# VectorE's share of the softmax exponentials: due passes ahead of the pass that waits for scores, and a higher threshold for taking score banks in the last layer

## The chip, the core and the metric

One core of a Trainium2 chip. The metric is the device time of one execution in microseconds; the kernel before takes 2177.55 us, the median of three runs (2173.53 to 2179.21).

## The reference

Four attention layers in a row on a tensor x of 2048 rows and 640 columns, 32 heads of 20 columns. Layers 0 and 2 look at a window of 256 keys (A), layers 1 and 3 at all 2048 keys (B).

```python
def _B_ref(x, wqkv, wo):
    qkv = (x @ wqkv).reshape(B, S, 3, H, Dh).transpose(2, 0, 3, 1, 4)
    q, k, v = qkv[0], qkv[1], qkv[2]
    scores = jnp.einsum("bhqd,bhkd->bhqk", q, k) * (Dh ** -0.5)
    p = _softmax(scores, axis=-1)
    o = jnp.einsum("bhqk,bhkd->bhqd", p, v)
    return o.transpose(0, 2, 1, 3).reshape(B, S, D) @ wo
# _A_ref: the same with scores masked to 0 <= q - k < 256
x = x + _A_ref(_layernorm(x), A_wqkv, A_wo)
x = x + _B_ref(_layernorm(x), B_wqkv, B_wo)
x = x + _A_ref(_layernorm(x), A_wqkv, A_wo)
x = x + _B_ref(_layernorm(x), B_wqkv, B_wo)
```

## The kernel before

The Python program writes every engine's instruction list out by hand. Queries come in 4 chunks of 512 rows (c), heads in 8 groups of 4 (g). A unit is one layer, chunk and group; a unit of a full layer has 64 score banks (16 blocks of 128 keys by 4 heads), and a bank is 128 keys by 512 queries, one of the eight PSUM banks. The main loop goes in steps (`tick`). Each step takes two to four banks from the current unit, issues their score matmuls (L1405), one ScalarE exponential over all of them (L1429), then the value matmuls of an earlier step (L1462) and a share of background work. Even steps use banks 0 to 2, odd ones 3 to 5 (and 6, where a step is four banks wide), bank 7 collects the output. Bank 6 is otherwise the one bank that the background shares (`take_m`, `drop_m`): layer norms, projections, the softmax denominators (`t_tail`: L1134, L1154, L1175) and output projections (`t_out`: L583). Each of these fills the bank with TensorE and has VectorE read it out. Idle places of TensorE are filled with matmuls that nobody reads (`unread`, in the profile as `ps<-masks,ident`).

ScalarE does most of the exponentials, and VectorE does a few in arithmetic of its own, two banks at a time: two fixed-point passes that read the scores from PSUM (`side_fixed`, L981, one for each bank), and then a chain on both banks: fraction (L997), square (L1005), cubic (L1009) and whole (L1015). In layer 1 the last two are cut in halves of 512 columns. Up to the first part of layer 3 (before `final`, the first unit of layer 3 with c = 1) the side bank is the third bank of a step's tile, whose exponential then covers two banks. From `final` on, `side_scores` computes it in bank 6 (L964), and the step keeps its three banks. `side["late"]` is set late in layer 3's first chunk.

Whether a step takes a side bank is decided by `state["lag"]`, the program's own account of how far VectorE is behind: each issued pass adds its length, each step takes off its ScalarE time. The account must be under `LAG` (late) or `LAG_1` (before). Chain passes are issued at the end of each step by `side_work(False)`, as long as the account stays within `WORK` or `WORK_1`. So in VectorE's order a fixed-point pass stands ahead of the chain passes of its own step.

Of the kernel before, what the change touches and what calls it, by code (L numbers as in the profile page):

```python
# [26 lines left out]
C = 512  # L27
# [9 lines left out]
LOG2E = 1.4426950408889634  # L37
T1, T0, TB = 3.219389291006841e-05, 3.290376630637895, -33.6189874849745
KA = 18
LAG = 0.5  # L40
LAG_1 = 0.5
WORK = 2.2
WORK_1 = 1.4
KEEP = 30
HALF = True
MOST_1 = 64
GAP_1 = 5
QA = 4
# [8 lines left out]
def kernel(  # L57
# [79 lines left out]
    def packed(l, c):  # L137

        return l == 3 and c > 0
# [55 lines left out]
    ready = set()  # L195
    todo = []
    tails = []
    state = {"tick": 0, "held": None, "credit": 0.0, "early": True, "act": True, "unit": 0, "heat": 0.0, "carry": 0.0, "least": 0.0, "floor": 0.0, "owed": 0, "lag": 0.0}

    class Task:  # L200

# [48 lines left out]
    def choose(blocked, limit=1 << 30):  # L250
        if state["held"] is not None:
            return state["held"]
        for t in tails:
            if t.wake <= state["tick"]:
                return t
        if not blocked:
            for t in todo:
                if t.wake <= state["tick"] and (t.need <= limit or t.holds):
                    return t
        return None  # L260
# [13 lines left out]
    mfree = {5: (0, 0), 6: (0, 1)}  # L274
    mseq = [1]

    def take_m():
        while True:
            b = min(mfree, key=mfree.get)
            if mfree[b][0] <= state["tick"]:  # L280
                mfree[b] = (1 << 30, 0)
                return b
            yield ("wait", 1)

    def drop_m(b):
# [9 lines left out]
    def require(what):  # L295
        n = 0
        while what not in ready:
            n += 1
            assert n < 100000, what
            t = choose(False, state["unit"] if n < 400 else 1 << 30)  # L300
            if t is None:
                state["tick"] += 1
                continue
            state["credit"] = max(state["credit"] - advance(t), -1.0)
# [444 lines left out]
    early = deque(Unit(1, 0, g, p) for p in PARTS[1][:3] for g in range(G))  # L749
# [109 lines left out]
    def finish_unit(u):  # L859
        l, c, g = u.l, u.c, u.g  # L860
        state["lag"] += 0.7
        if u.part and u.part[1] < NT:
            if not part_o:
                part_o["t"] = big.tile([P, G, C], F32, name="raw_o", tag="early_late")
            raw_o = part_o["t"][:, g, :]
            if u.part[0] == 0:
                nc.vector.tensor_copy(out=raw_o, in_=op)
            else:
                nc.vector.tensor_tensor(out=raw_o, in0=raw_o, in1=op, op=ALU.add)
            return  # L870
        if (l, c) not in ons:
            for ll, cc in list(ons):
                if len(ons) >= 2:
                    require(("out", ll, cc))
            ons[l, c] = onp.tile([P, G, C], BF16, name="on", tag="on")
        while len(tails) >= 3:
            require(tails[0].name)
        end = (l, c) == (3, NC - 1) and g >= G - 2
        oT = ons[l, c][:, 5 + g % 3 if packed(l, c) and not end else g, :]
        if u.part:  # L880
            nc.vector.tensor_tensor(out=oT, in0=part_o["t"][:, g, :], in1=op, op=ALU.add)
        else:
            nc.vector.tensor_copy(out=oT, in_=op)  # L883
        ended_units.append((l, c, g, oT))
        if len(ended_units) == 2 or g == G - 1 or end :
            push_tail(("tail", l, c, g), t_tail(list(ended_units)))
            ended_units.clear()
# [4 lines left out]
    side = {  # L892
        "xi": deque(), "chain": deque(), "out": deque(), "late": False, "early": False,
        "half": None, "at": 0, "last": 0,
    }
# [29 lines left out]
    def side_giver():  # L925
# [9 lines left out]
        for n in range(side["at"], min(side["at"] + 3, len(givers))):  # L935
# [3 lines left out]
            if not side["late" if u.l == 3 else "early"]:  # L939
                return None  # L940
            if u.l == 1 and len(u.aside) >= MOST_1:
                continue
            if len(u.rest) >= (KEEP if len(u.rest) + len(u.aside) < u.size else 12):
                side["at"] = n
# [13 lines left out]
    def side_scores(u):  # L958

        mseq[0] += 1  # L960
        mfree[6] = (state["tick"] + 2, mseq[0])
        kc, j = side_take(u)
        z = ps[:, 6, :]
        nc.tensor.matmul(z, lhsT=u.k(kc, j), rhs=u.q(j, 0, 4), start=True, stop=True)  # L964
        side_fixed(z)

    def side_fixed(z):

        u, a, b = side["half"]
        i = 0 if b is not None else 1  # L970
        if i == 0:
            side["now"] = side["xi"].popleft()
            side["half"] = (u, b, None)
        else:
            side["half"] = None
            if id(u) in deferred:
                live["kt"] -= 1
                live["qt"] -= 1
        xi = side["now"]
        side["last"] = state["tick"]  # L980
        nc.vector.tensor_scalar(  # L981
            out=xi.bitcast(I32)[:, i * C : (i + 1) * C], in0=z,
            scalar1=SCALE * LOG2E * FIX, scalar2=127.5 * FIX, op0=ALU.mult, op1=ALU.add,
        )
        state["lag"] += 0.7
        if i == 1:
            side["chain"].append(chain(u, xi))

    def chain(u, xi):

        V = nc.vector
        t = side["t"]
        low = xi.bitcast(I16)[:, 0::2]
        box = {}

        def fraction(h):
            V.tensor_scalar(  # L997
                out=t[:, h], in0=low[:, h], scalar1=T1, scalar2=T0, op0=ALU.mult, op1=ALU.add
            )

        def square(h):
            if "out" not in box:
                box["out"] = side["out"].popleft()
            q = box["q"] = box["out"].rearrange("p a b -> p (a b)").bitcast(F16)
            V.tensor_tensor(out=q[:, h], in0=t[:, h], in1=t[:, h], op=ALU.mult)  # L1005

        def cubic(h):
            q = box["q"]
            V.scalar_tensor_tensor(  # L1009
                out=q[:, h], in0=q[:, h], scalar=TB, in1=t[:, h], op0=ALU.add, op1=ALU.mult  # L1010
            )

        def whole(h):
            q = box["q"]
            V.scalar_tensor_tensor(  # L1015
                out=q.bitcast(U16)[:, h], in0=xi.bitcast(I32)[:, h], scalar=1.0 / C,
                in1=q[:, h], op0=ALU.mult, op1=ALU.add,
            )
            if h.stop == 2 * C:
                side["xi"].append(xi)  # L1020
                side_out.setdefault(id(u), []).append((box["out"], state["tick"]))

        every = (slice(0, 2 * C),)
        halves = (slice(0, C), slice(C, 2 * C)) if HALF and u.l == 1 else every
        cost = 0.7 if len(halves) == 2 else 1.25
        steps = [(fraction, h, 0.7) for h in every] + [(square, h, 0.7) for h in every]
        steps += [(cubic, h, cost) for h in halves] + [(whole, h, cost) for h in halves]
        return deque(steps)

    def side_work(force):  # L1030

        while side["chain"]:
            step, h, cost = side["chain"][0][0]
            if step.__name__ == "square" and not side["out"]:
                return False
            if not force and state["lag"] + cost > (WORK if side["late"] else WORK_1):
                return False
            side["chain"][0].popleft()
            if not side["chain"][0]:
                side["chain"].popleft()  # L1040
            step(h)
            state["lag"] += cost
            if force:
                return True
        return False
# [240 lines left out]
    with tc.manual_schedule():  # L1286
# [74 lines left out]
        while ended is None or t < ended + 8:  # L1361
            t += 1
            state["tick"] += 1
            n_b = 0
            if flow:
# [7 lines left out]
                if state["unit"] >= final:  # L1373
                    last_tick[0] = 0
                giver = side_giver() if state["lag"] < (LAG if side["late"] else LAG_1) else None
                if giver is not None and state["unit"] >= final and (
                    state["held"] is not None or mfree[6][0] > state["tick"]
                ):
                    giver = None
                cur = next_tile(t, giver)  # L1380
                n_b = len(cur)
                for b in cur:
                    u = b[0]
# [25 lines left out]
                if cur[-1][2] == "side":  # L1409
                    cur = cur[:-1]  # L1410
                    n_b -= 1
                    side_fixed(sp[:, n_b, :])
                elif giver is not None and state["unit"] >= final:
                    side_scores(giver)
                for b in cur:
                    if b[-1]:
                        s_emitted(b[0])
# [25 lines left out]
            for n in range(2 if n_b == 0 or t > closed + 1 else 0):  # L1443
                u = pts[0][3][0] if pts else None
# [6 lines left out]
                subs, end = group[0][3][4], group[-1][3][7]  # L1451
# [21 lines left out]
                if end:  # L1473
# [2 lines left out]
                    closed = t  # L1476
                    break

            if n_b and not state["early"]:
                background(t, n_b)  # L1480
            if n_b:
# [78 lines left out]
```

## Time and profile before

| what | value |
|---|---|
| median of three runs | 2177.55 us |
| the profiled execution | 2173.51 us |
| its span, first to last instruction | 2171.8 us |
| mean granted TensorE clock | 0.997 |
| side banks: layer 1, layer 3 (passes of L981 into raw_o, into xnT) | 112, 190 |

The span is the time from the first to the last instruction; about 1.7 us of the execution lie around it. Busy time is the union of an engine's spans, and a row's mean is that of single spans, which overlap: two exponentials that follow each other without a pause start 1.33 us apart, though each is recorded as some 1.5 us long. Layer 1 with layer 2 woven in takes about 450 to 1400 us of the span, layer 3's first chunk up to about 1540 us, and its other three chunks the rest.

### The profile page before, as it was taken

What the parts mean: (1) busy time and instruction counts of PE and PEld (TensorE: products, weight loads), DVE (VectorE), ACT (ScalarE), POOL (GpSimd) and SP (SyncE); (2) the same over time, 40 slices, a digit from 0 to 9 for tenths busy, and PEclk for the clock granted to TensorE, in tenths of its full rate; (3) what the DMA queues carried; (4) which work ended last, traced back from release to release, by engine and by line L of the source; (5) the groups of instructions that cost most, each with busy time, mean ns of one, the idle gap of its engine ahead of it and who ended that gap; (6) DMA issues with size and microseconds to landing.
All of it is one profiled execution on the core that took longest, in us unless ns stands there. A gap on an engine that the chain in (4) does not pass through costs nothing. (4 is left out here: it accounts for less than half of the span.)

```text
span 2171.8 us, 73321 instructions
## 1 busy us (share of the span) xinstructions
PE 1927.8 (89%) x31803; PEld 753.7 (35%) x31803; DVE 1443.6 (66%) x2564; ACT 2095.1 (96%) x1721; POOL 490.6 (23%) x952
## 2 busy tenths in 40 slices
PE   8899999988899888888988989888888888888888
PEld 4444443433333333333333433332222222222222
DVE  6656565426666676776777743676688778767876
ACT  7899899999999999999999999999999999999998
POOL 6665546110131213411053112511000000000000
PEclk9999999999999999999999999999999999999999
DMA  6233233332210323112241123122211111111100
GB/s 203 76 85 107 74 91 101 84 83 58 77 49 22 84 61 89 41 37 65 56 114 31 44 78 99 39 55 68 59 41 54 32 32 42 35 33 36 47 27 17
DMA packets 88418, 137.29 MB, mean 63 GB/s; under 512 B 20766, under 2 KB 63486, under 8 KB 88094
## 3 DMA queue, kind: packets, MB, share of 16 engines
q1 hardware_dynamic: 68878, 79.43, 13.8%
q0 software_dynamic: 19216, 53.17, 8.3%
q8 instruction: 249, 4.08, 0.8%
q14 instruction: 75, 0.61, 0.1%
HBM read 99.52 MB, written 27.79 MB: 59 GB/s over the span
## 5 line engine op out<-in xcount | busy, mean ns | idle before, releaser
L1429 ACT ACTIVATE pt<-ps 128x1536 bf16<-128x1536 f32 (+2 forms) x1641 | 2054.7, 1412 | 44.4 <-PE ps L1405 30.0
L1405 PE MATMUL ps<-qt,kt 32*128 32x512 bf16 x3930 | 546.1, 384 | 64.4 <-ACT pt L1429 57.0
L311 PE MATMUL ps<-masks,ident 128*32 128x512 bf16 x5696 | 503.4, 384 | 95.0 <-ACT pt L1429 50.4
L1462 PE MATMUL ps<-pt,vt 128*21 128x512 bf16 x3778 | 377.2, 386 | 0.5 <-ACT pt L1429 0.5
L1405 PEld LDWEIGHTS <-kt 32*128 32x128 bf16 x3930 | 156.2, 91 | 470.6 <-issue 452.1
L311 PEld LDWEIGHTS <-ident 128*32 128x32 bf16 x5696 | 178.4, 94 | 285.8 <-issue 259.0
L1500 POOL TENSOR_SCALAR_AFFINE_SELECT pt<-pt 128x256 bf16<-128x256 bf16 (+2 forms) x505 | 220.0, 458 | 189.4 <-ACT pt L1429 176.7
L311 PE MATMUL ps<-xnT,wqk 128*32 128x512 bf16 x3320 | 226.5, 382 | 10.5 <-DVE st L335 1.8
L981 DVE TENSOR_SCALAR xnT<-ps 128x512 int32<-128x512 f32 x190 | 131.0, 690 | 114.6 <-PE ps L964 108.7
L335 DVE CAST st<-ps 128x512 bf16<-128x512 f32 x134 | 92.6, 691 | 143.5 <-PE ps L311 143.2
L1462 PEld LDWEIGHTS <-vt 128*21 128x21 bf16 x3794 | 93.6, 89 | 252.8 <-issue 249.2
L311 PE MATMUL ps<-wop,on 128*32 128x320 bf16 x3712 | 160.5, 300 | 4.2 <-DVE x_sb L583 2.2
L311 PEld LDWEIGHTS <-on 128*32 128x32 bf16 x5760 | 122.3, 95 | 62.3 <-issue 29.1
L1511 DVE TENSOR_TENSOR pt<-pt,masks 128x512 bf16<-128x512 bf16 (+3 forms) x267 | 113.9, 442 | 42.5 <-ACT pt L1429 41.1
L1405 PE MATMUL ps<-qa,ka 32*128 32x256 bf16 (+2 forms) x1408 | 116.9, 275 | 23.6 <-ACT pt L1429 18.9
L311 PE MATMUL ps<-wv,xnT 128*32 128x320 bf16 x2560 | 116.4, 301 | 9.5 <-DVE vs L335 2.9
L583 DVE TENSOR_TENSOR x_sb<-x_sb,ps 128x320 bf16<-128x320 bf16 x120 | 58.3, 486 | 93.5 <-PE ps L311 92.6
L1175 DVE TENSOR_TENSOR on<-on,ps 128x512 bf16<-128x512 bf16 x128 | 86.2, 683 | 45.4 <-PE ps L311 43.9
L311 PEld LDWEIGHTS <-wqk 128*32 128x32 bf16 x3320 | 83.4, 96 | 94.6 <-issue 37.6
L981 DVE TENSOR_SCALAR raw_o<-ps 128x512 int32<-128x512 f32 x112 | 76.9, 686 | 37.9 <-PE ps L1405 36.7
L883 DVE CAST on<-ps 128x512 bf16<-128x512 f32 x112 | 76.7, 685 | 34.5 <-PE ps L1462 27.6
L550 POOL DMA_DIRECT2D k_d<-st x75 | 42.5, 567 | 223.5 <-DVE st L335 210.8
(101 smaller groups left out, 1757.5 us busy)
## 6 DMA issues: line engine op xcount, KB each, us to landing
vt<-v_d SPq DMA_DIRECT2D x48, 336.0 KB
kt<-k_d SPq DMA_DIRECT2D x192, 80.0 KB
wqk<-in_B_wqkv_dram POOLq DMA_DIRECT2D x80, 160.0 KB, 3.5
wqk<-in_A_wqkv_dram POOLq DMA_DIRECT2D x70, 160.0 KB, 3.6
k_d<-st POOLq DMA_DIRECT2D x75, 128.0 KB, 2.5
q_d<-st POOLq DMA_DIRECT2D x75, 128.0 KB, 2.3
qt<-q_d SPq DMA_DIRECT2D x384, 20.0 KB
v_d<-vs POOLq DMA_DIRECT2D x16, 336.0 KB, 3.0
```

The lines of the kernel that those rows point to most:

```text
L311: nc.tensor.matmul(out_[r], lhsT=lhsT[:, r], rhs=rhs, start=start, stop=stop)
L335: nc.vector.tensor_copy(out=out_, in_=in_)
L550: nc.gpsimd.dma_start(out=dst, in_=staging.pop())
L583: nc.vector.tensor_tensor(out=xv, in0=had, in1=yp, op=ALU.add)
L883: nc.vector.tensor_copy(out=oT, in_=op)
L981: nc.vector.tensor_scalar(out=xi.bitcast(I32)[:, i * C : (i + 1) * C], in0=z, scalar1=SCALE * LOG2E * FIX, scalar2=127.5 * FIX, op0=ALU.mu ...
L1175: nc.vector.tensor_tensor(out=oT, in0=oT, in1=zb, op=ALU.mult)
L1405: nc.tensor.matmul(sp[:, i, col * P : (col + qn) * P], lhsT=u.k(kc, j), rhs=u.q(j, q0, qn), start=True, stop=True,)
L1429: nc.scalar.activation(out=pt[:, i:k, b0 * P :], in_=sp[:, i:k, b0 * P :], func=ACT.Exp, scale=SCALE,)
L1462: nc.tensor.matmul(op[32 * j : 32 * j + VW, q0 * P : (q0 + qn) * P], lhsT=u.v(kc, j), rhs=pg[:, i, col * P : (col + qn) * P], start=(first ...
L1500: nc.gpsimd.affine_select(out=v, in_=v, compare_op=ALU.is_gt if later else ALU.is_ge, fill=0.0, base=0, pattern=[[0, k - i], [-1 if later ...
L1511: nc.vector.tensor_tensor(out=pt_[:, i:k, cols], in0=pt_[:, i:k, cols], in1=mv_, op=ALU.mult)
```

## The change

It does five things. `side_fixed` is preceded by a call of `side_work`, so that due chain passes go ahead of the fixed-point pass: with the limit `PRE` = 1.3 us in `side_scores` (late) and `PRE_1` = 0.8 us where the side bank is part of the tile. In the steps before `late` the background work of a step is preceded by the same call with `PRE_1`. `LAG` goes from 0.5 to 0.95. After `final`, a step takes no side bank where a background task has just asked for bank 6 in vain (`want`), or where starting a unit took the bank. And a unit in layer 3 with c > 0 requires the denominators of three (at the end two) units before it to be through, since it writes the same slot.

```diff
-LAG = 0.5
+LAG = 0.95
+PRE = 1.3
+PRE_1 = 0.8
+HALF_3 = False
@@ take_m
+            state["want"] = state["tick"]
             yield ("wait", 1)
@@ finish_unit
+        before = g - 2 if end else g - 3
+        if packed(l, c) and before >= 0:
+            require(("tail", l, c, before))
@@ side_scores
         nc.tensor.matmul(z, lhsT=u.k(kc, j), rhs=u.q(j, 0, 4), start=True, stop=True)
+        side_work(False, PRE)
         side_fixed(z)
@@ chain
-        halves = (slice(0, C), slice(C, 2 * C)) if HALF and u.l == 1 else every
+        halves = (slice(0, C), slice(C, 2 * C)) if HALF and (u.l == 1 or HALF_3) else every
@@ side_work
-    def side_work(force):
+    def side_work(force, limit=None):
+        if limit is None:
+            limit = WORK if side["late"] else WORK_1
...
-            if not force and state["lag"] + cost > (WORK if side["late"] else WORK_1):
+            if not force and state["lag"] + cost > limit:
@@ main loop
                 if giver is not None and state["unit"] >= final and (
                     state["held"] is not None or mfree[6][0] > state["tick"]
+                    or state["want"] >= state["tick"] - 1
                 ):
                     giver = None
...
+                    side_work(False, PRE_1)
                     side_fixed(sp[:, n_b, :])
                 elif giver is not None and state["unit"] >= final:
-                    side_scores(giver)
+                    if mfree[6][0] <= state["tick"]:
+                        side_scores(giver)
...
+            if n_b and not side["late"]:
+                side_work(False, PRE_1)
             if n_b and not state["early"]:
                 background(t, n_b)
```

More of the change, by code (lines that the diff above doesn't have):

```diff
@@ L197 @@
     tails = []
-    state = {"tick": 0, "held": None, "credit": 0.0, "early": True, "act": True, "unit": 0, "heat": 0.0, "carry": 0.0, "least": 0.0, "floor": 0.0, "owed": 0, "lag": 0.0}
+    state = {"tick": 0, "held": None, "credit": 0.0, "early": True, "act": True, "unit": 0, "heat": 0.0, "carry": 0.0, "least": 0.0, "floor": 0.0, "owed": 0, "lag": 0.0, "want": 0}
     class Task:
```

## The prediction

> **What bounds the kernel now.** I read the page's busy row and its costliest groups first, then ScalarE's groups with shapes kept apart, then three stretches of the span, then the waits of the last stretch.
>
> ```profile
> span 2171.8 us, 73321 instructions
> PE 1927.8 (89%) x31803; PEld 753.7 (35%) x31803; DVE 1443.6 (66%) x2564; ACT 2095.1 (96%) x1721; POOL 490.6 (23%) x952
> ...
> L1429 ACT ACTIVATE pt<-ps 128x1536 bf16<-128x1536 f32 (+2 forms) x1641 | 2054.7, 1412 | 44.4 <-PE ps L1405 30.0
> ...
> L981 DVE TENSOR_SCALAR xnT<-ps 128x512 int32<-128x512 f32 x190 | 131.0, 690 | 114.6 <-PE ps L964 108.7
> ```
>
> ScalarE (ACT) is busy for 2095.1 of 2171.8 us, and nearly all of it is the exponential. So time is saved by taking exponentials off ScalarE, or by ending what little idle time it has. VectorE (DVE) stood idle for 114.6 us ahead of layer 3's fixed-point passes, with nothing else allowed past them in its order. By stretches (columns: length, then busy time of PE, PEld, DVE, ACT, POOL, clock, DMA):
>
> ```profile
> 450.00:1400.00 950.00, 839.12 (x14171) 341.77 (x14163) 603.00 (x1168) 939.69 (x751) 230.59 (x422) 1.00 0.23 62
> 1400.00:1500.00 100.00, 89.12 (x1402) 35.18 (x1391) 81.99 (x128) 94.23 (x77) 18.38 (x27) 1.00 0.23 62
> 1500.00:2150.00 650.00, 574.71 (x7803) 179.54 (x7802) 492.08 (x653) 646.00 (x479) 0.00 (x0) 1.00 0.14 38
> ```
>
> In the last 650 us ScalarE is busy for 646.0 and VectorE for 492.1. Stalls of ScalarE there are worth only 4 us, or a little more: in the shapes of 1500 to 2140 us there are 465 exponentials of three banks, 4 of four and 2 of two. At the start-to-start times below (1.33, 1.76 and 0.90 us, the last by the same slope) they need 627 of 640 us, so some 13 us are lost to short delays that the spans hide. Layers 1 and 2 have 10 us idle and some hidden delays more. These are all that a better order could win back.
>
> **The banks that change engine.** I counted both kernels' instructions in the order in which they stand. ScalarE loses 4 exponentials of 2048 columns and 4 of 1536 and gains 4 of 1024: 20 banks fewer, all in layer 3 (fixed-point passes into xnT go from 190 to 210; into raw_o, layer 1, they stay at 112). Four of them come out of tiles before `final`, 16 are side banks in bank 6. What ScalarE spends on a bank shows where shapes follow each other:
>
> ```profile
> 1733.34 2.87 ACT L1429 ACTIVATE pt<-ps 128x1536 bf16<-128x1536 f32 x2
> 1736.00 1.98 ACT L1429 ACTIVATE ka<-ps 128x2048 bf16<-128x2048 f32 x1
> 1737.76 2.91 ACT L1429 ACTIVATE pt<-ps 128x1536 bf16<-128x1536 f32 x2
> ```
>
> Two exponentials of 1536 columns take (1736.00 - 1733.34) / 2 = 1.33 us each, one of 2048 takes 1737.76 - 1736.00 = 1.76, so a bank is 0.43 us. The sum is 4 x 1.76 + 4 x 0.43 = 8.8 us less for ScalarE. By recorded durations (1975, 1530 and 1072 ns) it would be 4 x 1.975 + 4 x 0.458 = 9.7; I take the starts, since the spans overlap.
>
> The Trainium skill, page "ScalarE: Activation LUTs", section "What ACT_TABLE_LOAD costs", gives an exponential with a pointer bias about 280 ns plus 0.833 ns a column, 93 ns of which overlap with the next. As an estimate by that page four instructions of 2048 columns would free 4 x 1.893 us, and with four banks of 0.427 the sum would be 9.3; the trace's 1.76 us is shorter than the page's 1.89, and the trace is used.
>
> **What VectorE gains in work.** Ten chains more: 2 x 0.690 (L981) + 0.694 (L997) + 0.692 (L1005) + 1.224 (L1009) + 1.217 (L1015) = 5.2 us each, 52 us in all, 8 of the chains after `final`. In the last stretch VectorE goes from 492 to about 534 of some 642 us, 83%. It is not the bound as long as the work lies in its idle time. The cover is the 114.6 us ahead of L981. By the order, 74 of 190 of these passes had a chain pass directly ahead, 125 such passes in all; now 155 of 210, 274 passes in all. At the durations above that is 129.7 us before and 270.2 now: 140 us are moved or added in front of passes that leave 114.6 us of idle time. So up to 26 us are not covered, and fixed-point passes end later by that much in sum, 0.12 us each. Who waits for a late one is the next writer of bank 6, which the program lets in two steps later, 2 x 1.33 = 2.66 us; the pass itself takes 0.69. A delay of 0.12 us in the mean costs nothing, and single ones of one chain pass (1.22 us) still fit. So I cost it at nothing, up to 26 us if each were felt.
>
> **TensorE and bank 6.** The score and value matmuls are the same in number; 20 value matmuls only move from one line to another, and 16 score matmuls from L1405 to L964, and 44 filler matmuls go. TensorE's waits after 1500 us:
>
> ```profile
> PE ps L964 <- DVE on L1175: 9.1, 23, 0.7
> PE ps L964 <- DVE x_sb L583: 6.9, 23, 0.7
> ...
> PE ps L964 <- DVE rz L1134: 1.4, 6, 0.4
> ```
>
> A side bank waits here for VectorE to read out what the background left in bank 6, 17.4 us in 52 waits (columns: total, times, longest). Scores of the next step stand behind it, so these are the source of some of the 13 us above. The last pass other than chain passes ahead of a fixed-point pass was L1175 or L583 52 times and is 44 times now; and chain passes directly ahead of all L583 and L1175 go from 181 to 123, so the bank is read out earlier. Eight waits at 17.4 / 52 = 0.33 us are 2.7 us of TensorE, of which I give ScalarE a third, 1 us. Bounds: half of the 13 us of hidden delays, 6 us, won, or, with 182 instead of 166 passes of L964 and a backlog allowed up to 0.95 instead of 0.5, 4 us lost (each of some 40 such waits longer by 0.3 us, and a third of that felt). The test for `want` and the test of bank 6 before `side_scores` add no instruction; the new `require` finds its units done and issues nothing ahead of time.
>
> **Layers 1 and 2.** The side banks are as many as before. Of 381 read-outs by VectorE between the first and the last side bank of layer 1, 109 had chain passes directly ahead and 101 have now; ahead of the 112 fixed-point passes stand 104 chain passes instead of 114. The cover of a pass put ahead of a projection is VectorE's own wait for it: L335 into st was waited for 143.5 us over 134 passes, 1.07 us each, against 0.69 for a half chain pass. What if it isn't there: TensorE waits 0.4 us a time on L335 now (11.8 us, 29 times, from 500 to 1450 us). I take 0, from 4 us won to 4 us lost, a tenth of the roughly 35 us of TensorE waits on VectorE there. GpSimd's and SyncE's transfers keep their number (1479 on SyncE's queue), and the tail after the last exponential (it ends at 2161.3 of 2171.8 us) has the same work.
>
> **Sum.** 2171.8 - 8.8 - 1 = 2162.0 us of span, 1.7 us around it as now: 2163.7 against the profiled 2173.5. The median of the runs is 4.0 us above that execution, so 2167.8, say 2168 us.
>
> **Rivals.**
> 1. The gain is eaten by new short waits (within 0.3%). For it: the taking of banks has been made bolder by a threshold, and all of ScalarE's slack in the last stretch is one tile; its 13 us of hidden delay come from waits of 0.3 to 0.7 us on bank 6. Against it: only 0.6 us of TensorE time in the whole trace waits for a fixed-point pass. If the 17.4 us of waits grow by two thirds and half of that arrives, with half the bound of layers 1 and 2: -8.8 + 5.8 + 2 = -1, 2176.
> 2. Slower: VectorE's order. A chain pass of 1.22 us in front of the fixed-point pass holds it, bank 6 stays full, L964 waits, and with it the next tile's scores on TensorE. The uncovered 26 us would all be felt: 2177.55 - 8.8 + 26 = 2195. It decides from 8.8 / 26, a third of the lateness, on. For it: VectorE at 83%. Against: the 2.66 us before the bank is asked for again.
>    The Trainium skill, page "PSUM — Partial Sum Buffer", section "Engine vs sequencer instructions", says that VectorE's queue is strictly first in, first out, which is what this rival needs; the trace agrees, with VectorE idle for up to 3.0 us ahead of L981.
> 3. More than forecast: both bounds of the small terms fall on the good side, -8.8 - 6 - 4 = -18.8, 2159.
> That the change does not do what it says is out as to the counts, which were taken from the instructions.
>
> **How the numbers follow.** Forecast 0.55, more than forecast 0.10, eaten 0.23, slower 0.12. The measurement of this kernel can tell 0.3%, 6.5 us, from no change. Faster by more than that: rival 3 and the forecast but for a tenth of it that misses the 6.5 us, 0.60, and a little of the eaten case, 0.03: 0.63. Within: 0.25. Slower: 0.12. The range goes from rival 3, 2159, to rival 1, 2176, and leaves rival 2 and a share of rival 1 out. The forecast's own range is 2162 to 2173.
>
> **What would show it.** Exponentials: 1280 of 1536 columns, 280 of 1024, none of 2048, and ScalarE's busy time near 2086 us. VectorE near 1495 us, its idle time ahead of L981 into xnT well under half of 114.6 us. Waits of L964 on L1175 and L583 at or below 16 us. The forecast is wrong if TensorE waits for L981 by several us, if ScalarE's busy share in the last stretch falls under 98.5%, or if its idle time between 450 and 1500 us grows by over 5 us.

## The result, and the profile after

The changed kernel takes 2169.51 us (median of 21 runs, 2165.04 to 2175.66), the kernel before 2173.7 (21 runs, 2169.25 to 2179.21). The ratio is 0.998, with a 95% interval of 0.9973 to 0.9987: a gain of 4.2 us that is clear of the noise and less than half of the 9.8 us forecast (8.8 for the banks and 1 for shorter waits). The profiled execution took 2167.19 us, its span is 2165.5.

The page of the changed kernel, its busy row and the groups of the exponential and of the fixed-point passes (L1442 is the old L1429, L1416 the old L1405, L989 the old L981, L971 the old L964, L315 the old L311; VectorE's read-outs are L339 of projections, the old L335, L587 of output projections, the old L583, and L1185 at the end of the denominators, the old L1175; in the versions below some of these lines stand one or two earlier):

```profile
span 2165.5 us, 73279 instructions
...
PE 1924.8 (89%) x31759; PEld 754.6 (35%) x31759; DVE 1488.7 (69%) x2625; ACT 2086.1 (96%) x1717; POOL 485.9 (22%) x953
...
L1442 ACT ACTIVATE pt<-ps 128x1536 bf16<-128x1536 f32 (+2 forms) x1641 | 2051.7, 1406 | 46.4 <-PE ps L1416 35.5
...
L989 DVE TENSOR_SCALAR xnT<-ps 128x512 int32<-128x512 f32 x210 | 144.1, 687 | 34.6 <-PE ps L971 27.5
```

ScalarE's busy time falls by 9.0 us, but the span by 6.3: ScalarE is idle for 2.7 us more. VectorE's idle time ahead of L989 into xnT falls from 114.6 to 34.6 us. The stretches tell where ScalarE lost time (columns: length, then busy time of PE, PEld, DVE, ACT, POOL, clock, DMA; first the kernel before, then the changed one):

```profile
450.00:1395.00 945.00, 834.75 (x14085) 339.88 (x14077) 599.69 (x1159) 934.69 (x747) 227.15 (x415) 1.00 0.23 63
1395.00:1540.00 145.00, 127.25 (x2060) 49.83 (x2056) 99.50 (x165) 139.18 (x111) 21.81 (x35) 1.00 0.23 61
1540.00:2140.00 600.00, 531.45 (x7094) 163.66 (x7088) 469.61 (x613) 596.05 (x440) 0.00 (x0) 1.00 0.13 37
```

```profile
450.00:1395.00 945.00, 835.47 (x14104) 340.51 (x14103) 602.68 (x1165) 936.17 (x749) 224.25 (x419) 1.00 0.23 63
1395.00:1540.00 145.00, 124.05 (x1986) 48.61 (x1985) 105.49 (x170) 135.09 (x109) 20.82 (x33) 1.00 0.22 58
1540.00:2140.00 600.00, 537.86 (x7197) 167.80 (x7190) 512.70 (x676) 597.02 (x443) 0.00 (x0) 1.00 0.13 38
```

Before 1395 and after 1540 us ScalarE is as busy as it was, or 1 us more so. From 1395 to 1540 us, where layer 3's first chunk runs beside the last projections, it is busy for 135.1 instead of 139.2 us. In the kernel before, ScalarE's waits of that stretch and the largest of TensorE's waits for a read-out were these (total, times, longest):

```profile
ACT pt L1429 <- PE ps L1405: 2.4, 6, 0.6
ACT pt L1429 <- PE ps L1462: 2.2, 2, 1.4
ACT pt L1429 <- PE ps L1055: 0.7, 1, 0.7
```

```profile
PE ps L311 <- DVE st L335: 1.9, 3, 0.9
```

In the changed kernel they are:

```profile
ACT pt L1442 <- PE ps L1416: 9.5, 16, 1.3
```

```profile
PE ps L315 <- DVE x_sb L587: 2.8, 4, 1.3
PE ps L315 <- DVE st L339: 2.7, 4, 1.4
PE ps L315 <- DVE vs L339: 2.4, 4, 1.2
PE ps L315 <- DVE on L1185: 1.5, 1, 1.5
```

So ScalarE waits for 9.5 us there instead of 5.3. TensorE's waits for VectorE add up to 11.6 us instead of 6.1, and the longest of them is 1.5 us instead of 0.9. One of the waits in the changed kernel's timeline (start, length, what; in brackets the idle time before it and what ended it):

```profile
1420.39 1.22 DVE L1023 SCALAR_TENSOR_TENSOR ka<-xnT,ka 128x1024 uint16<-128x1024 int32 x1
...
1421.67 1.19 PE L315 MATMUL ps<-wop,on 128*32 128x320 bf16 x24
1421.74 0.69 DVE L989 TENSOR_SCALAR xnT<-ps 128x512 int32<-128x512 f32 x1
...
1422.35 0.48 DVE L406 BATCH_NORM_STATS2 stats<-x_sb 128x6 f32<-128x320 bf16 x1
...
1422.75 0.48 DVE L407 BATCH_NORM_STATS2 stats<-x_sb 128x6 f32<-128x320 bf16 x1
...
1423.39 0.64 DVE L871 COPY raw_o<-ps 128x512 f32<-128x512 f32 x1
...
1423.94 0.47 DVE L587 TENSOR_TENSOR x_sb<-x_sb,ps 128x320 bf16<-128x320 bf16 x1
...
1424.47 0.32 PE L315 MATMUL ps<-wop,on 128*32 128x320 bf16 x4 [1.28 <-DVE x_sb L587]
...
1425.43 1.02 ACT L1442 ACTIVATE pt<-ps 128x1024 bf16<-128x1024 f32 x1 [0.66 <-PE ps L1416]
```

The output projection had filled bank 6 by 1422.9 us. VectorE had done a chain pass (L1023) and the fixed-point pass, was still behind with the statistics and a unit's output, and began to read the bank out at 1423.94. TensorE waited 1.28 us for that, the scores behind it came late, and ScalarE stood for 0.66 us.

### The profile page after: what moved, and what is told of

It reads as the page before. It is cut to its first block, busy times and chain, and to the rows that moved or that the text cites. A ratio compares the mean times of both kernels' runs of the same rounds, so it can differ in the third digit from the quotient of the medians.

```text
span 2165.5 us, 73279 instructions
## 1 busy us (share of the span) xinstructions
PE 1924.8 (89%) x31759; PEld 754.6 (35%) x31759; DVE 1488.7 (69%) x2625; ACT 2086.1 (96%) x1717; POOL 485.9 (22%) x953
## 5 line engine op out<-in xcount | busy, mean ns | idle before, releaser
L1442 ACT ACTIVATE pt<-ps 128x1536 bf16<-128x1536 f32 (+2 forms) x1641 | 2051.7, 1406 | 46.4 <-PE ps L1416 35.5
L1416 PE MATMUL ps<-qt,kt 32*128 32x512 bf16 x3914 | 544.6, 383 | 59.8 <-ACT pt L1442 52.5
L315 PE MATMUL ps<-masks,ident 128*32 128x512 bf16 x5652 | 505.6, 384 | 96.6 <-ACT pt L1442 47.5
L1416 PEld LDWEIGHTS <-kt 32*128 32x128 bf16 x3914 | 154.7, 91 | 460.2 <-issue 440.4
L315 PEld LDWEIGHTS <-ident 128*32 128x32 bf16 x5652 | 180.3, 94 | 278.9 <-issue 253.5
L315 PE MATMUL ps<-xnT,wqk 128*32 128x512 bf16 x3320 | 225.2, 381 | 11.9 <-DMA wqk<-in_B_wqkv_dram 2.1
L339 DVE CAST st<-ps 128x512 bf16<-128x512 f32 x134 | 92.5, 690 | 143.9 <-PE ps L315 143.6
L989 DVE TENSOR_SCALAR xnT<-ps 128x512 int32<-128x512 f32 x210 | 144.1, 687 | 34.6 <-PE ps L971 27.5
L315 PE MATMUL ps<-wop,on 128*32 128x320 bf16 x3712 | 160.5, 300 | 5.7 <-DVE x_sb L587 3.9
L1526 DVE TENSOR_TENSOR pt<-pt,masks 128x256 bf16<-128x256 bf16 (+3 forms) x268 | 113.4, 438 | 46.5 <-ACT pt L1442 44.3
L315 PEld LDWEIGHTS <-on 128*32 128x32 bf16 x5760 | 122.3, 95 | 63.7 <-issue 29.8
L1416 PE MATMUL ps<-qa,ka 32*128 32x384 bf16 (+2 forms) x1408 | 118.0, 276 | 22.5 <-ACT pt L1442 19.1
L587 DVE TENSOR_TENSOR x_sb<-x_sb,ps 128x320 bf16<-128x320 bf16 x120 | 58.2, 485 | 101.6 <-PE ps L315 101.1
L1185 DVE TENSOR_TENSOR on<-on,ps 128x512 bf16<-128x512 bf16 x128 | 86.4, 684 | 59.2 <-PE ps L315 57.0
L315 PE MATMUL ps<-wv,xnT 128*32 128x320 bf16 x2560 | 116.0, 301 | 9.0 <-DVE vs L339 2.0
L315 PEld LDWEIGHTS <-wqk 128*32 128x32 bf16 x3320 | 83.2, 96 | 96.0 <-issue 38.1
L989 DVE TENSOR_SCALAR raw_o<-ps 128x512 int32<-128x512 f32 x112 | 76.8, 686 | 47.3 <-PE ps L1416 46.8
```

The lines of the kernel that those rows point to most:

```text
L315: nc.tensor.matmul(out_[r], lhsT=lhsT[:, r], rhs=rhs, start=start, stop=stop)
L339: nc.vector.tensor_copy(out=out_, in_=in_)
L587: nc.vector.tensor_tensor(out=xv, in0=had, in1=yp, op=ALU.add)
L989: nc.vector.tensor_scalar(out=xi.bitcast(I32)[:, i * C : (i + 1) * C], in0=z, scalar1=SCALE * LOG2E * FIX, scalar2=127.5 * FIX, op0=ALU.mu ...
L1185: nc.vector.tensor_tensor(out=oT, in0=oT, in1=zb, op=ALU.mult)
L1416: nc.tensor.matmul(sp[:, i, col * P : (col + qn) * P], lhsT=u.k(kc, j), rhs=u.q(j, q0, qn), start=True, stop=True,)
```

## The experiments

Theory A: a bank off ScalarE pays 0.43 us, the threshold of 0.95 brings all the banks, and the missing part of the gain is lost in layer 3's first chunk, where banks are taken while VectorE is behind. Theory B gives the loss or the gain to the order of VectorE's passes. Each expectation says what A and B mean for its version. The edits are against the changed kernel unless said otherwise; ratios are to the kernel before.

**The threshold from `final` on alone.**

```diff
-giver = side_giver() if state["lag"] < (LAG if side["late"] else LAG_1) else None
+giver = side_giver() if state["lag"] < (LAG if state["unit"] >= final else LAG_1) else None
```

> The changed kernel, with the threshold of 0.95 only from `final` on and 0.5 before it; 208 passes of L989 into xnT (before the change 190, changed kernel 210), so 18 banks off ScalarE. Theory A (the banks pay 0.43 us each, and the missing half of the gain is lost in layer 3's first chunk, where banks were taken with VectorE up to 0.9 us behind): ScalarE's idle time from 1395 to 1540 us falls from 9.5 back to about 5 us, and the time is 18 x 0.43 = 7.7 us under the kernel before, a ratio of 0.9965. Theory B (the missing half is lost to chain passes put ahead of projections, or of fixed-point passes): the idle time there stays near 9.5 us and the ratio near 0.998.

Measured: 2162.8 us, ratio 0.9956 (0.9942 to 0.9969). ScalarE's waits from 1395 to 1540 us are 5.0 us, its busy time there 139.36:

```profile
ACT pt L1442 <- PE ps L1475: 2.2, 2, 1.3
ACT pt L1442 <- PE ps L1416: 2.1, 5, 0.6
ACT pt L1442 <- PE ps L1065: 0.7, 1, 0.7
```

Theory A holds: with two banks fewer on VectorE this version is faster than both kernels, by 0.44% against the kernel before.

**The same stretch in the kernel before.** Here the kernel before gets the higher threshold only where the last experiment took it away.

```diff
-giver = side_giver() if state["lag"] < (LAG if side["late"] else LAG_1) else None
+giver = side_giver() if state["lag"] < (0.95 if side["late"] and state["unit"] < final else LAG_1) else None
```

> The kernel before with one edit: the threshold is 0.95 between `late` and `final`, that is in layer 3's first chunk, and 0.5 elsewhere. 194 passes of L981 into xnT, so 4 banks off ScalarE, 1.7 us. Theory A (VectorE's backlog at the moment a bank is taken delays its read-outs for the projections there): ScalarE's idle time from 1395 to 1540 us goes from 5.3 to about 9.5 us, ratio 1.001 to 1.002. Theory B (that idle time has another source in the changed kernel): idle time near 5.3 us and ratio 0.999.

Measured: ratio 1.001 (1.0001 to 1.0019), 2.9 us slower, although four banks left ScalarE. The interval reaches from 0.2 to 4.1 us, so the time alone says little. The waits say more: ScalarE's wait for scores there is 9.4 us, and TensorE's four largest waits for VectorE are those of the changed kernel to the digit. Two of them:

```profile
ACT pt L1429 <- PE ps L1405: 9.4, 16, 1.3
```

```profile
PE ps L311 <- DVE x_sb L583: 2.8, 4, 1.3
PE ps L311 <- DVE st L335: 2.7, 4, 1.4
```

So the threshold in that stretch is enough to bring these waits, with nothing else of the change, and without it (last experiment) they are gone. What no run separates is whether they come from taking a bank while VectorE is further behind, or simply from the two more chains that VectorE has to do there (104.5 us busy instead of 99.5).

**No pass put ahead.** The three calls of `side_work` ahead of other work are left out.

```diff
-        side_work(False, PRE)
         side_fixed(z)
...
-                    side_work(False, PRE_1)
                     side_fixed(sp[:, n_b, :])
...
-            if n_b and not side["late"]:
-                side_work(False, PRE_1)
```

> The changed kernel without the three calls that put chain passes ahead; the threshold and the rest stay. 210 passes into xnT, as in the changed kernel. Theory A (the threshold alone brings the banks, the order of VectorE's passes is worth next to nothing): ratio 0.998, like the changed kernel, although VectorE idles some 100 us again ahead of the fixed-point passes. Theory B (without the order VectorE cannot carry 20 banks more, and they are paid back in waits on bank 6): ratio 1.000 to 1.004, with over 25 us of TensorE waits at L971 for VectorE.

Measured: 0.9985 (0.9976 to 0.9994), like the changed kernel. The time is theory A's; one number of mine in it, some 100 us of VectorE's idle time, was wrong. The idle time does not come back:

```profile
L988 DVE TENSOR_SCALAR xnT<-ps 128x512 int32<-128x512 f32 x210 | 144.3, 688 | 39.8 <-PE ps L971 32.8
```

It is 39.8 us, against 34.6 with the calls. The threshold ended the idle time (with the calls and `want` but the old threshold, further below, it is 139.0 us): a bank taken while VectorE is 0.7 us behind finds chain passes of the step before already in front. In the order 261 chain passes stand directly ahead of the 210 fixed-point passes without the calls, 274 with them. So the calls move only 13 passes.

**No calls, threshold from `final` on alone.** Both edits above together.

> 0.95 from `final` on alone, with the `want` test, and without any of the calls that put chain passes ahead. 208 passes into xnT, 18 banks off ScalarE, as in the version with those calls, which measured 0.9956. Theory A (the order is worth nothing at this threshold, since at a backlog of 0.7 us a pass of 0.7 exceeds the limit of 1.3): 0.995 to 0.9965. Theory B (the calls help where the backlog is low): 0.998 or above.

Measured: 2162.93 us, 0.9952 (0.9939 to 0.9964), the same as with the calls. The calls are worth nothing measurable here.

**Order alone, at the banks of before.**

```diff
-LAG = 0.95
+LAG = 0.5
...
-                    or state["want"] >= state["tick"] - 1
```

> The changed kernel with the threshold at 0.5 and without the `want` test: 190 passes into xnT, 112 into raw_o and every exponential as in the kernel before; what is left of the change is the order of VectorE's passes. Theory A (the order is worth nothing): ratio 0.999 to 1.001, and VectorE's idle time ahead of the passes into xnT stays over 100 us. Theory B (passes ahead fill that idle time, as the prediction's sum of the cover has it): idle time under 60 us, ratio 0.998 or below.

Measured: 0.999 (0.9982 to 0.9999), at the edge of no change, with a gain of up to 0.18% left possible. VectorE's idle time is untouched:

```profile
L989 DVE TENSOR_SCALAR xnT<-ps 128x512 int32<-128x512 f32 x190 | 130.8, 689 | 114.4 <-PE ps L971 108.9
```

The trace also shows why: 128 chain passes stand directly ahead of the 190 fixed-point passes, against 125 in the kernel before. At the old threshold there is hardly a due pass that the calls could put ahead. So this run shows that these calls are worth next to nothing, and not that the order of passes could not matter.

**Passes ahead, at the old threshold.** `LAG = 0.5`, the rest as changed.

> The changed kernel with the threshold back at 0.5: the passes go ahead, but only 166 passes into xnT, 24 banks fewer on VectorE than before the change, and 12 exponentials of 2048 columns. Theory A: 24 x 0.43 = 10.3 us slower than the kernel before, ratio 1.0047. Theory B (the order itself shortens waits): clearly less, ratio 1.002 or below.

Measured: 2184.86 us, 1.0057 (1.0044 to 1.0069), by the ratio 12.4 us slower where 24 banks at 0.43 us make 10.3. Compared with the last experiment the difference is the `want` test: it turns 24 banks away at this threshold.

**Layers 1 and 2 as before.** Only the two calls with `PRE_1` are left out.

> The changed kernel without the two calls with the 0.8 us limit, so that layers 1 and 2 are issued as before the change; 210 passes into xnT. Theory A: no difference to the changed kernel, ratio 0.998. Theory B (passes ahead of projections cost what the banks bring): ratio 0.996, with ScalarE's idle time from 450 to 1400 us near the 10.3 us of before and that from 1395 to 1540 us near 5 us.

Measured: 0.9983 (0.9975 to 0.9992), no difference from the changed kernel; ScalarE waits 9.1 us for L1416 from 1395 to 1540 us. The passes ahead of projections cost nothing measurable.

**Without `want`.** The threshold from `final` on alone, and the line `or state["want"] >= state["tick"] - 1` left out.

> The version with 0.95 from `final` on alone, without the `want` test: 222 passes into xnT, 32 banks off ScalarE against the kernel before, 14 more than with the test. Theory A (a bank off ScalarE pays 0.43 us as long as TensorE's waits on VectorE stay short): 32 x 0.43 = 13.8 us, ratio 0.9936. Theory B (the background that is turned away from bank 6 is late, and the units behind it wait): not under the 0.9956 of the version with the test, and TensorE's waits for VectorE after 1540 us well over its 15 us.

Measured: 2246.1 us, 1.0333 (1.0318 to 1.0347). ScalarE's busy time is lower than in any other version, 2082.5 us, and it waits for 85.8 us after 1540 us:

```profile
ACT pt L1441 <- PE ps L1415: 85.8, 35, 9.4
```

```profile
PE ps L315 <- DVE x_sb L587: 19.9, 8, 3.9
PE ps L315 <- DVE on L1185: 16.1, 21, 0.8
PE ps L315 <- DMA wop<-in_B_wo_dram: 9.6, 1, 9.6
PE ps L315 <- DMA on<-on: 4.7, 2, 4.2
```

Theory B holds here. The background does not get bank 6 in time and then runs in one piece, with its waits for VectorE and for transfers in front of the scores. Between 1641.5 and 1649.4 us, for example, TensorE computes no scores but softmax denominators (and filler), waits seven times for VectorE, and ScalarE stands for 6.66 us; one wait for the output weights alone is 9.6 us. The granted TensorE clock was 0.94 from 1540 to 2140 us, against 1.00 in the kernel before, so a part of the loss may be slower matmuls; no run separates the two.

**Every due pass ahead.** The threshold from `final` on alone, with `PRE = 9.0`.

> The version with 0.95 from `final` on alone, with PRE = 9 instead of 1.3, so that every due chain pass goes ahead of the fixed-point pass in bank 6; 206 passes into xnT, 16 banks off ScalarE against the kernel before. Theory A (bank 6 is asked for again two steps later, so a late fixed-point pass is not felt): 16 x 0.43 = 6.9 us, ratio 0.9968. Theory B (the prediction's slower rival: a late pass holds the bank and TensorE behind it): TensorE waits for L989 appear, over 10 us, and the ratio is 1.000 or above.

Measured: 2192.72 us, 1.0087 (1.0073 to 1.0101), although 16 banks left ScalarE. TensorE's waits after 1540 us:

```profile
PE ps L971 <- DVE xnT L989: 25.1, 49, 1.0
PE ps L971 <- DVE x_sb L587: 8.5, 24, 0.9
PE ps L315 <- DVE xnT L989: 5.4, 9, 0.8
```

25.1 + 5.4 = 30.5 us are waits for the fixed-point pass, which in the changed kernel are 0.3 us. ScalarE's wait after 1540 us:

```profile
ACT pt L1442 <- PE ps L1416: 24.8, 62, 1.8
```

The Trainium skill, page "PSUM — Partial Sum Buffer", section "Engine vs sequencer instructions", describes VectorE's queue as strictly first in, first out; the waits on L989 agree with it. The slower rival's mechanism is real, and the limit of 1.3 us keeps the changed kernel out of it.

**The changed kernel again**, on the same chip as the version with the first chunk's threshold alone and the one without calls.

> The changed kernel as it is, on the same chip as the two others: 0.998 by both theories, and 4 to 6 us slower than the version with 0.95 from `final` on alone.

Measured: 2171.0 us, 0.9988 (0.9979 to 0.9997), 8.1 us slower than the version without calls and with the threshold from `final` on alone, on the same chip. That is more than the 4 to 6 us expected. ScalarE's wait for scores from 1395 to 1540 us is 11.7 us in its trace.

## Why the prediction was right in part

**The banks: right.** 20 banks, 0.43 us each. ScalarE's busy time went to 2086.1 us where 2086 was named, and the two versions with 18 banks fewer and without the threshold in the first chunk gain 9.6 us (0.9956) and 10.4 us (0.9952). 18 x 0.43 = 7.7 us and the 1 us given to shorter waits make 8.7, which lies within both intervals (6.7 to 12.6 and 7.8 to 13.3 us).

**Bank 6 after `final`: right in size, as far as can be told.** L971's waits on L1185 and L587 are 12.0 us in the changed kernel (16.0 before), but 2.7 us of TensorE waits came back at L315. The stretch from 1540 to 2140 us has 597.0 us of ScalarE instead of 596.1, but single profiles scatter by as much: the version with the order alone, which has the waits of before (9.2 and 6.9 us), has 597.5. The calls have no part in it: without them the waits of L971 on these two read-outs are 12.0 us as well.

**Layers 1 and 2: right.** Taken as 0; ScalarE was busy 1.5 us longer from 450 to 1395 us, but 1.9 us longer in the kernel before with the first chunk's threshold alone, whose program is the same up to there, so this is scatter between profiles. Leaving the calls out changes nothing that can be measured.

**Layer 3's first chunk: this step failed.** The prediction followed the threshold only into bank 6 after `final`, and gave "Layers 1 and 2", whose projections run beside that chunk, a term of 0 and a bound of 4 us for passes put ahead. It had no term for the threshold there. In that chunk the fixed-point pass goes in front of read-outs that a projection waits for, and the threshold decides how much VectorE may have in front of it already: 0.95 us by the program's account instead of 0.5. ScalarE stood 4.2 us longer in it in the trace of the changed kernel, and 6.4 us longer in that of its repeat. By time, the isolated edit cost 2.9 us with four banks saved (1.7 us), so the waits cost 4.6. On the same chip, the versions with the threshold in this chunk were 6.5 and 8.1 us slower than those without it (2169.25 against 2162.8, 2171.0 against 2162.93), although they have two banks more off ScalarE (0.9 us), so 7.4 to 9.0. Part of the 3 to 4 us between the two figures lies after 1540 us. ScalarE is busy there, up to 2140 us, for 596.1 to 597.1 us in the four traces with both parts of the threshold and for 598.5 in both versions that have it from `final` on alone, and TensorE waits for a read-out of the denominators, first in the changed kernel, then in the version with the threshold from `final` on alone:

```profile
PE ps L315 <- DVE on L1185: 3.0, 9, 0.5
```

```profile
PE ps L315 <- DVE on L1185: 0.2, 1, 0.2
```

Why the first chunk's threshold brings these later waits is open, and so is the rest, which lies near the reach of the intervals. The prediction's own signs of being wrong did not show this loss: TensorE's wait for L989 is 0.3 us, ScalarE's share in the last stretch is 99%, and its idle time from 450 to 1500 us grew by only 1.9 us, since ScalarE stood longer in the first chunk but less in the layers before it.

**VectorE's idle time: right number, wrong reason.** "Well under half of 114.6 us" came true with 34.6. The prediction's cover sum counted the 274 chain passes ahead of L981 without asking which part of the change put them there. 261 of them stand there without any call. The calls at the old threshold leave 114.4 us of idle time; the new threshold without the calls leaves 39.8.

**The outcome is that of the first rival** in size, a gain within 0.3%, which had a chance of 0.23, while the forecast had 0.55. That rival was right that the bolder threshold would bring new short waits, but it laid most of them (5.8 us) to bank 6 after `final` and 2 us to layers 1 and 2; most of the loss was in layer 3's first chunk. That the median came within 1.5 us of the predicted 2168 is luck, owed to two misses that nearly cancel: the gain was 5.6 us smaller than forecast, and the kernel before took 3.9 us less over 21 runs than over the first three.

**`want`: priced as nothing, worth 3%.** "Add no instruction" was true. But at a threshold of 0.95 it is what keeps the background running: without it 14 banks more leave ScalarE, and 83.3 us are lost between the two versions (2246.1 against 2162.8, measured on two chips).

## What to carry to other kernels

A threshold that lets more work onto an engine with time to spare should be priced in each stretch where it applies: where that engine's next job is to free a shared buffer for the bottleneck's supplier, even a small backlog can arrive at the bottleneck. Here 0.45 us more of it, and two more chains, cost ScalarE 4.2 us of 145. Where two parts of a change could both explain a filled gap, build each alone before naming the one; the calls that put passes ahead looked like the cause here, and they moved 13 passes of 274 and did nothing measurable. And a rule that only says no (the test for a waiting background task) can be the part that makes the rest possible: without it the same version is 3.3% slower than the kernel before, and with it 0.4% faster.

## What the runs showed of the hardware

In the changed kernel the spread of 10 us between runs goes with the granted clock of TensorE: of its 21 runs, those with a mean clock of 0.997 or more took 2165.0 to 2169.6 us, those at 0.994 and under 2171.2 to 2175.7. In the kernel before the link is weaker: measured beside the repeat, its four runs at 0.998 took 2169.9 to 2174.1 us, and one at 0.995 took 2169.8. Which of the two, clock or waits, brings the other is not shown. In the profile of the version with the first chunk's threshold alone the first 450 us had a clock of 0.98 and 399.1 us of ScalarE, against 0.99 and 404.0 in the kernel before. A few microseconds between the spans of two single profiles are therefore no evidence. The stretches above were compared at clocks of 0.99 to 1.00, but for the version without `want` (0.94 after 1540 us) and the repeat of the changed kernel (0.98 from 1395 to 1540 us).
